# Two chunks of all four sequences in a group, instead of eight chunks of one sequence, in a chunked recurrence with a mixture of experts behind it

## The chip, the cores and the metric

The kernel runs on one core of a Trainium2 chip. The metric is the time of one execution on the device in microseconds; the median of three runs is compared.

## What is computed

A complex linear recurrence with a decay for each channel, read out by a query, and a mixture of experts with one expert per token behind it. Cut to what matters:

```python
B, H, S, D = 4, 8, 768, 48
scale = min(mag, 0.999) / (mag + 1e-6)          # mag = |a_re + i a_im|
for t in range(S):
    S_re, S_im = ar * S_re - ai * S_im + k[t] v[t]^T, ar * S_im + ai * S_re
    y[t] = q[t] @ S_re                           # for each sequence b and head h
x = y as 3072 tokens of 384
# 8 experts of 384 -> 1024 -> 384, argmax gate, capacity 768 rows an expert
out[i] = gate[i] * relu(x[i] @ w1[e]) @ w2[e]
```

## The kernel before

**Chunks.** Each sequence is cut into 8 chunks of 96 positions. Inside a chunk the products of decays from the chunk's middle outward are made by a scan; queries and keys are multiplied by them, and the chunk is then a small attention (scores, mask, times values) plus the contribution of a state `z` from the chunks before. A new state is made for the next chunk: S (keys times values, on TensorE) plus the old `z`, then a complex multiplication by the decay across the two chunk halves.

**Groups and stages.** The scan works on 128 partitions at once. These hold one group: one sequence, its 8 heads times 8 chunks, forward and backward from the middle (2 x 64 rows). A group has 6 tiles of 8 positions. `norm` (L246 on) loads `a` and normalises it, `scan` does two VectorE instructions a position (L362, L367), `post` (L381 on) multiplies the queries and keys and writes them to `scr` in DRAM. `pend` (L454 on) takes the decay at the scan's end, transposes it and makes `pcol`, the decays from one chunk to the next (L498 to L503). Stage g is the time of group g's scan.

**Units.** While group g+1 is scanned, the 8 chunks of group g go through `unit` (L507 on), one after the other. A unit loads `qkc` back from `scr` in two parts (480 KB and 90 KB, L524), the centre row and `v`, transposes (L542), makes the scores `pa` (L558), masks them to `a_sb` (L562), makes y (L614, and L619 with the state), and passes y to the router. For the state it does S (L572), the add on VectorE (L579 for the first chunk, L581 else), a copy of the sum with its partition halves swapped, as two transfers issued by SP (L585, tile `sx`), eight small multiplications on ScalarE (L590, tile `u`), `sx` times `pcol` on VectorE (L593, the update's first half) and their sum into the next state (L596, second half). The add of chunk c+1 reads the state made by chunk c.

**Routing and experts.** When a group's units are through, its tokens get experts and slots (`routing`), and their rows are sent to `disp`. In the last group this is done after 5 units and then unit by unit. Then the first expert's inputs are put together (L912, L918), and the experts run (L1032, L1040).

**The order.** Nearly all of this is recorded as operations of a planner (`Plan`): each has an engine, an estimated duration, the operations it comes after, the buffers it needs and a time `want` at which it is wanted. `solve` goes through them greedily and writes an order for each engine; the hardware then runs each engine's instructions in that order, so that one that waits holds up all behind it on its engine. The landing of a transfer is estimated in `solve` from its size and the queue (`o.lat`). `RINGS` has the number of buffers for each kind of tile, `BEGIN` the planned beginnings of the stages.

```python
x = [plan.op(None, "SP", .55, lambda i=i: swap(i), w - 20, after=[d], ..., kb=72) for i in range(2)]
u = plan.op(None, "ACT", 1.8, turn, w + 4 * f, after=[d, ("pc", b)], ...)
za = plan.op(None, "DVE", dve(384), state_a, w + 5 * f, after=x + [("pc", b)], ...)
plan.op(K("ZB"), "DVE", dve(384), state_b, w + 6 * f, after=[u, za], ...)
```

Here `d` is the add, `w` the time planned for the unit and `f` a ninth of the time planned for one unit.

Of the kernel before, what the change touches and what calls it, by code (L numbers as in the profile page):

```python
# [7 lines left out]
F32 = mybir.dt.float32  # L8
# [13 lines left out]
NC = S // C  # L22
SIZES = (8,) * 6
# [22 lines left out]
class Plan:  # L46
# [25 lines left out]
    def solve(self, slack=.13, late=8.):  # L72
# [30 lines left out]
        while left:  # L103
# [52 lines left out]
class Att:  # L156


    def __init__(self, const, c_att, tc, dram, ident, av, xv, cen, vp):
# [10 lines left out]
        self.sums = [const.tile([128, 2, NSUM], F32, name=f"sums{g}") for g in range(B)]  # L170
# [4 lines left out]
        for t in self.sums:  # L175
# [16 lines left out]
        self.col = [0] * B  # L192
# [53 lines left out]
    def norm(self, g, j, s0):  # L246
# [16 lines left out]
        plan.op(K + ("load",), eng, .6, load, w - 14, bufs=[a_], kb=48 * n)  # L263
# [117 lines left out]
    def post(self, g, j, e0):  # L381
# [11 lines left out]
        plan.op(K + ("load",), "POOL" if g else "SP", .6, load, w - 14, bufs=[i_], kb=48 * n)  # L393
# [60 lines left out]
    def pend(self, g, want):  # L454
# [31 lines left out]
        def copy():  # L486
            vg = st['vg'] = self.p_t.tile([C, 2, 2, H, NC], F32, tag="vg", name=f"vg_{g}", bufs=1)
            nc.scalar.copy(out=vg.rearrange("p z s h c -> p (z s h c)"), in_=st['pt'][:, :256])
        o = plan.op(None, "ACT", act(256), copy, want, after=[o], bufs=[("tr", K)])

        def cols():
            vg = st['vg']
            pr = self.p_t.tile([C, 2, H, NC], F32, tag="vgp", name=f"vgp_{g}", bufs=1)
            p = self.pcol[g]
            s1, s0 = slice(1, NC), slice(0, NC - 1)
            V = lambda z: vg[:, z, 0, :, s1]
            G = lambda z: vg[:, z, 1, :, s0]
# [3 lines left out]
            nc.vector.tensor_tensor(out=pr[:, 1, :, s1], in0=V(0), in1=G(1), op=ALU.mult)
            nc.vector.tensor_tensor(out=p[:, 0, :, s1], in0=p[:, 0, :, s1], in1=pr[:, 0, :, s1], op=ALU.add)
            nc.vector.tensor_tensor(out=p[:, 1, :, s1], in0=p[:, 1, :, s1], in1=pr[:, 1, :, s1], op=ALU.subtract)  # L503
        plan.op(("pc", g), "DVE", 6 * dve(56) + .2, cols, want + 2, after=[o])
# [914 lines left out]
```

## Time and profile before

| | us |
|---|---|
| median of three runs (725.82 to 727.86) | 727.04 |
| the profiled execution | 719.15 |
| its span, first to last instruction | 717.4 |
| TensorE matmul busy | 598.5 (83%) |
| VectorE busy | 468.8 (65%) |
| ScalarE busy | 383.4 (53%) |
| GpSimd busy | 160.1 (22%) |

All rows come from the profiled execution. Times in it count from the span's start. PE is TensorE's matmuls, PEld its weight loads, DVE VectorE, ACT ScalarE, POOL GpSimd, SP the engine that issues most transfers; a q behind a name is that engine's sequencer, which issues transfers. A busy share of the whole run mixes stages with different limits, so the stretches have to be looked at one by one.

### The profile page before, as it was taken

What the parts mean: (1) busy time and instruction counts of PE and PEld (TensorE: products, weight loads), DVE (VectorE), ACT (ScalarE), POOL (GpSimd) and SP (SyncE); (2) the same over time, 40 slices, a digit from 0 to 9 for tenths busy, and PEclk for the clock granted to TensorE, in tenths of its full rate; (3) what the DMA queues carried; (4) which work ended last, traced back from release to release, by engine and by line L of the source; (5) the groups of instructions that cost most, each with busy time, mean ns of one, the idle gap of its engine ahead of it and who ended that gap; (6) DMA issues with size and microseconds to landing.
All of it is one profiled execution on the core that took longest, in us unless ns stands there. A gap on an engine that the chain in (4) does not pass through costs nothing. (4 is left out here: it accounts for less than half of the span.)

```text
span 717.4 us, 12886 instructions
## 1 busy us (share of the span) xinstructions
PE 598.5 (83%) x4545; PEld 506.4 (71%) x4545; DVE 468.8 (65%) x1369; ACT 383.4 (53%) x1002; POOL 160.1 (22%) x231
## 2 busy tenths in 40 slices
PE   4445487968997777979658998999999999999994
PEld 1222176856886556767558886899999999999993
DVE  4999976878997886978635454345437454554721
ACT  7655475867786685767428642333426334352610
POOL 8124331122261221711212021002021111202012
PEclk9565578998999988989858988999999999999998
DMA  5368986767887666775688512643026707261601
GB/s 176 88 205 237 272 252 201 188 152 186 199 248 207 155 167 146 203 229 136 151 182 218 138 54 73 194 129 127 13 66 194 224 28 225 65 193 55 203 25 39
DMA packets 75929, 111.92 MB, mean 156 GB/s; under 512 B 7739, under 2 KB 65970, under 8 KB 75856
## 3 DMA queue, kind: packets, MB, share of 16 engines
q1 hardware_dynamic: 61904, 63.17, 32.8%
q0 software_dynamic: 13952, 47.84, 23.3%
q8 instruction: 38, 0.62, 0.4%
q14 instruction: 35, 0.29, 0.1%
HBM read 73.18 MB, written 34.46 MB: 150 GB/s over the span
## 5 line engine op out<-in xcount | busy, mean ns | idle before, releaser
L958 DVE TENSOR_TENSOR lo<-raw,hi 128x384 fp32r<-128x384 f32 (+2 forms) x128 | 65.0, 554 | 43.5 <-ACT hi L957 43.3
L1077 DVE SCALAR_TENSOR_TENSOR hl<-ph,hh 128x448 fp32r<-128x448 f32 x64 | 39.9, 623 | 70.7 <-ACT hh L1076 70.7
L957 ACT CAST hi<-raw 128x384 fp32r<-128x384 f32 (+2 forms) x128 | 59.0, 512 | 50.3 <-DMA raw<-in_moe_w_dram 27.7
L1076 ACT ACTIVATE hh<-ph 128x448 fp32r<-128x448 f32 x64 | 34.2, 545 | 88.1 <-PE ph L1032 88.0
L542 PE MATMUL tr<-ident,qkc 96*96 96x96 f32 x512 | 63.9, 265 | 20.7 <-issue 6.4
L240 PE MATMUL n<-a,ident 128*128 128x384 f32 x92 | 48.4, 665 | 35.7 <-ACT a L268 33.6
L542 PEld LDWEIGHTS tr<-ident,qkc 96*96 96x96 f32 x512 | 50.6, 136 | 28.8 <-issue 13.9
L1032 PE MATMUL ph<-xl,hi 128*128 128x448 f32 x192 | 70.6, 368 | 0.0
L1032 PE MATMUL ph<-xh,hi 128*128 128x448 f32 x192 | 70.5, 372 | 0.0
L1032 PE MATMUL ph<-xh,lo 128*128 128x448 f32 x192 | 69.9, 364 | 0.0
L240 PE MATMUL p<-qko,ident 128*128 128x384 f32 x96 | 47.5, 629 | 23.3 <-ACT qko L399 23.3
L1006 POOL DMA_INDIRECT out_dram<-o,xr x28 | 26.3, 941 | 180.2 <-DVE o L1005 175.9
L558 PE MATMUL pa<-qT,kT 128*96 128x96 f32 x512 | 58.5, 262 | 6.7 <-ACT kT L546 5.4
L362 DVE TENSOR_TENSOR xy<-a 128x192 f32<-128x192 f32 (+1 forms) x215 | 62.0, 306 | 1.6 <-ACT a L332 1.5
L590 ACT ACTIVATE u<-s,pcol 96x48 f32<-96x48 f32 x224 | 53.6, 324 | 16.8 <-DVE s L581 15.8
L1040 PE MATMUL my<-hh,lo 128*128 128x448 f32 x168 | 61.2, 364 | 0.0
L1040 PE MATMUL my<-hl,hi 128*128 128x448 f32 x168 | 61.1, 364 | 0.0
L558 PEld LDWEIGHTS pa<-qT,kT 128*96 128x96 f32 x512 | 53.2, 177 | 10.2 <-ACT kT L546 6.4
L240 PEld LDWEIGHTS n<-a,ident 128*128 128x128 f32 x92 | 21.1, 251 | 53.0 <-ACT a L268 35.2
L1040 PE MATMUL my<-hh,hi 128*128 128x448 f32 x168 | 56.0, 372 | 0.0
L614 PE MATMUL y<-a_sb,v 128*64 128x96 f32 x512 | 45.1, 266 | 12.6 <-DVE a_sb L562 12.6
L859 POOL DMA_INDIRECT disp<-x,idx x32 | 34.1, 1067 | 89.5 <-DVE sx L593 41.6
(192 smaller groups left out, 1374.4 us busy)
## 6 DMA issues: line engine op xcount, KB each, us to landing
raw<-in_moe_w_dram SPq DMA_DIRECT2D x64, 384.0 KB
qkc<-scr SPq DMA_DIRECT2D x32, 480.0 KB
scr<-qko POOLq DMA_DIRECT2D x24, 384.0 KB, 4.0
scr<-qko POOLq DMA_DIRECT2D x40, 192.0 KB, 5.3
a<-in_av_dram POOLq DMA_DIRECT2D x18, 384.0 KB, 5.5
qkin<-in_xv_dram POOLq DMA_DIRECT2D x18, 384.0 KB, 7.7
disp<-fill POOLq DMA_DIRECT2D x7, 772.0 KB, 8.7
xr<-disp SPq DMA_DIRECT2D x8, 675.5 KB
```

The lines of the kernel that those rows point to most:

```text
L240: nc.tensor.matmul(out=pt[:, :m], lhsT=self.ident, rhs=t[:, h:h + m], start=i == 0, stop=i == 1)
L362: nc.vector.tensor_tensor(out=st['xy'][:, :, cs].rearrange("p (u z) d -> p u z d", u=2), in0=a4[:, s, :, cs].rearrange("p (u z) d -> p u z ...
L542: nc.tensor.transpose(out=pt[:, h * C:h * C + C], in_=qk[:C, 4 * hh + h, z_ * C:z_ * C + C], identity=self.ident[:C, :C])
L558: nc.tensor.matmul(out=pa[:, h * C:h * C + C], lhsT=kT[:, 4 * hh + h], rhs=qT[:, 4 * hh + h], start=True, stop=True)
L590: nc.scalar.mul(out=u[:, h, :], in_=st['s'][:, h, :], mul=pc[:, 0, h, c + 1:c + 2])
L614: nc.tensor.matmul(out=py[o:o + DP, i // 2 * C:i // 2 * C + C], lhsT=v[:, h * D:h * D + DP], rhs=a_sb[:, h, :], start=True, stop=c == 0)
L957: return (lambda: nc.scalar.copy(out=hi[i][:, s], in_=raw[i][:, s]), lambda: nc.vector.tensor_tensor(out=lo[i][:, s], in0=raw[i][:, s], in ...
L958: lambda: nc.vector.tensor_tensor(out=lo[i][:, s], in0=raw[i][:, s], in1=hi[i][:, s].bitcast(F32), op=ALU.subtract))
L1032: nc.tensor.matmul(out=ph[:, :T], lhsT=a[:, k, fs], rhs=r[:, k], start=k == 0 and i == 0, stop=k == KT - 1 and i == 2)
L1040: nc.tensor.matmul(out=py[m][:, :T], lhsT=a[:, f % self.PF, ms], rhs=r, start=f == 0 and i == 0, stop=f == NF - 1 and i == 2)
L1076: nc.scalar.activation(hh, ph[:, :T], AF.Relu)
L1077: nc.vector.scalar_tensor_tensor(out=hl, in0=ph[:, :T], scalar=0.0, in1=hh.bitcast(F32), op0=ALU.max, op1=ALU.subtract)
```

## The change

A group no longer holds 8 chunks of one sequence but 2 chunks of all 4 sequences (group g has chunks 2g and 2g+1). The inputs are laid out for that on the host, as before for the old grouping. The units of a group go chunk 2g of the sequences 0 to 3 first and then chunk 2g+1 of the same. The state from chunk 2g+1 to 2g+2 needs the decays of two groups; its add, swap and S are done with the unit, and the two multiplications and the sum are finished in the next group's stage, after its scan. `pend` therefore makes `pcol` for each chunk of the group apart, with the tile `vg` of the group before. More states are kept: `z` has 6 buffers, the sum `s_sb` and its swapped copy `sx` 5 each; for this `a` and `qk` have 3 instead of 4, and `a4` has 4 instead of 5. The planner now counts 5 us more for the landing of a swap, 2 us more for the loads of `a` and `qk`, and 1 us more for those of `qkc`. Routing and the list of tokens follow the new order of units.

```diff
+NG = 4
+G2 = NC // NG
+NU = B * G2
-                o.lat = pipe[o.eng] + .5 - t - o.dur
+                o.lat = pipe[o.eng] + .5 + o.extra - t - o.dur
-        plan.op(K + ("load",), eng, .6, load, w - 14, bufs=[a_], kb=48 * n)
+        plan.op(K + ("load",), eng, .6, load, w - 14, bufs=[a_], kb=48 * n, extra=2.)
 def cols():
-            nc.vector.tensor_tensor(out=p[:, 0, :, s1], in0=V(0), in1=G(0), op=ALU.mult)
...
+            for i in range(int(g == 0), G2):
+                V = [self.vg[g][:, z, 0, :, i] for z in range(2)]
+                G = [self.vg[g - (i == 0)][:, z, 1, :, (i - 1) % G2] for z in range(2)]
+                p = [self.pcol[g][:, z, :, i] for z in range(2)]
+                nc.vector.tensor_tensor(out=p[0], in0=V[0], in1=G[0], op=ALU.mult)
...
-    def unit(self, b, c, w, per):
+    def unit(self, g, i, w, per, near):
-        n = NC * b + c
+        n = NU * g + i
+        b, c = i % B, G2 * g + i // B
+        zi = lambda c: (c - 1) * B + b
+        z, zn = buf("z", zi(c)), buf("z", zi(c + 1))
...
-            x = [plan.op(None, "SP", .55, lambda i=i: swap(i), w - 20, after=[d], bufs=[R("s_sb"), R("sx")], kb=72) for i in range(2)]
-            u = plan.op(None, "ACT", 1.8, turn, w + 4 * f, after=[d, ("pc", b)], bufs=[R("s_sb"), R("u")])
-            za = plan.op(None, "DVE", dve(384), state_a, w + 5 * f, after=x + [("pc", b)], bufs=[R("sx")])
-            plan.op(K("ZB"), "DVE", dve(384), state_b, w + 6 * f, after=[u, za], bufs=[R("sx"), R("u"), ("z", b, c + 1)])
+            x = [plan.op(None, "SP", .55, lambda i=i: swap(i), w - 20, after=[d], bufs=[R("s_sb"), R("sx")], kb=72, extra=5.) for i in range(2)]
+            pcn = ("pc", nx // G2)
+            wz = w + 12 * f if nx // G2 == g else near + 1.5 * b
+            u = plan.op(None, "ACT", 1.8, turn, wz, after=[d, pcn], bufs=[R("s_sb"), R("u")])
+            za = plan.op(None, "DVE", dve(384), state_a, wz, after=x + [pcn], bufs=[R("sx")])
+            plan.op(K("ZB"), "DVE", dve(384), state_b, wz + 2, after=[u, za], bufs=[R("sx"), R("u"), ("z", b, c + 1)])
...
-RINGS = dict(qkc=3, v=3, qT=3, kT=2, a_sb=2, z=3, s_sb=2, sx=2, u=2, xt=2, tr=2, pa=2, s=1, ad=2, y=1,
-             a=4, qk=4, a4=5, ln=4, c0=3, t5=3, xy=4, qko=4, pend=1)
+RINGS = dict(qkc=3, v=3, qT=3, kT=2, a_sb=2, z=6, s_sb=5, sx=5, u=2, xt=2, tr=2, pa=2, s=1, ad=2, y=1,
+             a=3, qk=3, a4=4, ln=4, c0=3, t5=3, xy=4, qko=4, pend=1)
...
+        for g in range(NG):
+            per = (BEGIN[g + 2] - BEGIN[g + 1]) / NU if g < NG - 1 else 7.05
+            for i in range(NU):
+                att.unit(g, i, BEGIN[g + 1] + 12 + per * i, per, BEGIN[min(g + 2, NG)] + 4)
```

The planner's order changes nearly everywhere. Three places matter here. Names carry first the sequence and the chunk for tiles of units (`s_1_4`: sequence 1, chunk 4), the group and the tile or position for tiles of the scan, and last a running number.

**VectorE, stage 2: from the add to the update's first half.** Before, sequence 1, chunk 4:

```order
L581 TENSOR_TENSOR s_1_4_2564<-s_1_4_2481,z1_126 96x384
L362 TENSOR_TENSOR xy_2_4_7_2574<-a4_2_4_2061,a4_2_3_1899 128x192
L562 TENSOR_TENSOR a_sb0_123<-pa_1_4_0_2558,mask_252 96x384
L367 TENSOR_TENSOR a4_2_4_2061<-xy_2_4_7_2574 128x2x24 x2
L362 TENSOR_TENSOR xy_2_4_6_2594<-a4_2_4_2061 128x4x24 x2
L367 TENSOR_TENSOR a4_2_4_2061<-xy_2_4_6_2594 128x2x24 x2
L562 TENSOR_TENSOR a_sb0_123<-pa_1_4_1_2585,mask_252 96x384
L362 TENSOR_TENSOR xy_2_4_5_2607<-a4_2_4_2061 128x192
L404 TENSOR_TENSOR qko_2_3_2581<-a4_2_3_1899,qkin_2_3_2320 128x8x96
L1255 TENSOR_SCALAR ok2_5405<-sums2_81 128x24
L367 TENSOR_TENSOR a4_2_4_2061<-xy_2_4_5_2607 128x96
L593 TENSOR_TENSOR sx_1_4_2565<-sx_1_4_2565,pcol1_109 96x384
```

In the changed kernel, chunk 2 of sequences 2 and 1:

```order
L586 TENSOR_TENSOR s_2_2_2355<-s_2_2_2263,z0_125 96x384
L323 SCALAR_TENSOR_TENSOR a4_2_3_1888<-a_2_3_1811,sign_93,t5n_2_3_1968 128x8x48
L598 TENSOR_TENSOR sx_1_2_2181<-sx_1_2_2181,pcol1_109 96x384
L327 TENSOR_TENSOR a4_2_3_1888<-a_2_3_1811,t5n_2_3_1968 128x8x48
L567 TENSOR_TENSOR a_sb0_123<-pa_2_2_0_2327,mask_254 96x384
L567 TENSOR_TENSOR a_sb0_123<-pa_2_2_1_2349,mask_254 96x384
L601 TENSOR_TENSOR z3_128<-u_1_2_2233,sx_1_2_2181 96x384
```

Before, the first half (L593) stands 11 rows behind the add of the same unit. In the changed kernel the add of sequence 2 (L586) is followed by the first half of sequence 1 (L598), whose own add stands 26 rows above; that of sequence 2 stands 21 rows below its add. Over stages 1 to 3 the distance is 7 to 13 rows before, with one of 27 (21 cases), and 16 to 94 in the changed kernel, median 44 (24 cases).

**VectorE, the last group: adds and updates.** Before, sequence 3, chunks 0 and 1:

```order
L579 COPY s_3_0_4406<-s_3_0_4375 96x384
L855 CAST idx_2_0_4365<-slot_2_0_4352 96x1 x2
L562 TENSOR_TENSOR a_sb0_123<-pa_3_0_0_4449,mask_252 96x384
L958 TENSOR_TENSOR lo1_0_0_4283<-raw1_0_0_4279,hi1_0_0_4281 128x384 x2
L562 TENSOR_TENSOR a_sb0_123<-pa_3_0_1_4471,mask_252 96x384
L593 TENSOR_TENSOR sx_3_0_4407<-sx_3_0_4407,pcol3_111 96x384
L596 TENSOR_TENSOR z0_125<-u_3_0_4431,sx_3_0_4407 96x384
L581 TENSOR_TENSOR s_3_1_4531<-s_3_1_4420,z0_125 96x384
```

In the changed kernel, chunk 6 of sequences 1, 0, 2 and 3:

```order
L586 TENSOR_TENSOR s_1_6_4589<-s_1_6_4525,z3_128 96x384
L867 CAST idx_2_0_4553<-slot_2_0_4540 96x1 x5
L970 TENSOR_TENSOR lo1_0_1_4365<-raw1_0_1_4361,hi1_0_1_4363 128x384 x2
L598 TENSOR_TENSOR sx_0_6_4467<-sx_0_6_4467,pcol3_111 96x384
L601 TENSOR_TENSOR z0_125<-u_0_6_4489,sx_0_6_4467 96x384
L586 TENSOR_TENSOR s_2_6_4658<-s_2_6_4609,z4_129 96x384
L970 TENSOR_TENSOR lo0_0_2_4412<-raw0_0_2_4408,hi0_0_2_4410 128x256
L567 TENSOR_TENSOR a_sb1_124<-pa_1_6_0_4653,mask_254 96x384
L970 TENSOR_TENSOR lo1_0_2_4413<-raw1_0_2_4409,hi1_0_2_4411 128x384 x2
L567 TENSOR_TENSOR a_sb1_124<-pa_1_6_1_4678,mask_254 96x384
L586 TENSOR_TENSOR s_3_6_4747<-s_3_6_4712,z5_130 96x384
```

Before, the next add (L581) reads the state `z0` that the row above it has made. In the changed kernel the adds read `z3`, `z4` and `z5`, which were finished before the group's units began; the state `z0` made here is for chunk 7.

**SP, the loads of the last group's first units and the first expert weights.** `qkc` from `scr3_1` is the large part, which needs the first five tiles of the group, from `scr3_0` the small part, which needs the last one; `raw` are weights, which go where the scan's tiles were and so wait for the scan's last transfers. Before:

```order
L948 DMA raw0_0_0_4278<-in_moe_w1_dram 128x3x256
L528 DMA qkc2_114<-in_cen_dram 1x1536
L948 DMA raw0_0_1_4297<-in_moe_w1_dram 128x3x256
L524 DMA qkc2_114<-scr3_1_103 80x8x192
L524 DMA qkc0_112<-scr3_0_102 15x8x192
```

In the changed kernel:

```order
L533 DMA qkc2_114<-in_cen_dram 1x1536
L529 DMA qkc2_114<-scr3_1_103 80x8x192
L960 DMA raw0_0_0_4353<-in_moe_w1_dram 128x3x256
L960 DMA raw0_0_1_4360<-in_moe_w1_dram 128x3x256
L536 DMA v2_117<-in_vp_dram 96x384
L529 DMA qkc0_112<-scr3_0_102 15x8x192
```

The third unit's large part has moved ahead of the weights, out of the place between them and the first unit's small part.

## Rows read from the trace of the kernel before

**Rows 1.** Busy time by engine in seven stretches of the span: begin and end, length, busy us and number of instructions of PE, PEld, DVE, ACT and POOL, then the granted TensorE clock (1.00 is 2.4 GHz), the busy share of the DMA engines and GB/s. The first three are stages 1 to 3, then the gap before the tail, the tail, the first expert's inputs, the experts.

```profile
71.10:159.60 88.50, 65.84 (x617) 52.03 (x617) 70.43 (x234) 57.14 (x160) 22.07 (x32) 0.83 0.79 216
159.60:253.80 94.20, 81.09 (x842) 65.88 (x842) 81.82 (x251) 71.67 (x206) 30.52 (x40) 0.93 0.75 195
253.80:345.70 91.90, 76.55 (x800) 62.35 (x798) 77.08 (x245) 63.76 (x182) 26.94 (x34) 0.90 0.66 171
345.70:371.20 25.50, 13.12 (x114) 10.89 (x110) 12.19 (x45) 6.42 (x20) 2.61 (x4) 0.65 0.78 174
371.20:440.70 69.50, 62.65 (x744) 57.07 (x745) 36.20 (x131) 40.89 (x132) 15.12 (x15) 0.88 0.54 136
440.70:454.00 13.30, 13.30 (x49) 8.23 (x48) 2.86 (x19) 1.09 (x3) 0.92 (x1) 0.74 0.41 106
454.00:717.00 263.00, 252.97 (x1346) 234.66 (x1344) 127.03 (x242) 98.02 (x212) 31.38 (x32) 0.99 0.38 117
```

**Rows 2.** The timeline of ScalarE, the copy at the end of each scan (start, duration).

```profile
71.06 0.26 ACT L464 COPY pend<-a 128x96 f32<-128x96 f32 x1
...
159.57 0.28 ACT L464 COPY pend<-a 128x96 f32<-128x96 f32 x1
...
253.84 0.26 ACT L464 COPY pend<-a 128x96 f32<-128x96 f32 x1
...
345.65 0.25 ACT L464 COPY pend<-a 128x96 f32<-128x96 f32 x1
```

**Rows 3.** Who VectorE waited for, in three stretches (72 to 163, 163 to 254 and 254 to 350 us): us in total, times, the longest.

```profile
DVE sx L593 <- DMA sx<-s: 13.4, 3, 6.6
...
DVE sx L593 <- DMA sx<-s: 7.3, 3, 3.7
...
DVE sx L593 <- DMA sx<-s: 8.9, 4, 4.1
DVE s L579 <- PE s L572: 5.6, 1, 5.6
```

**Rows 4.** The instructions that write or read the swapped copy: duration least, median and most in ns, first and last start; and what VectorE waited for before them.

```profile
L593 DVE TENSOR_TENSOR sx<-sx,pcol x28: 541/553/555, 102.3 to 423.8; 96x384 f32<-96x384 f32 x28
L596 DVE TENSOR_TENSOR z<-u,sx x28: 542/554/614, 103.0 to 424.3; 96x384 f32<-96x384 f32 x28
...
  DMA sx<-s: 35.3, 12
```

**Rows 5.** The timelines of SP and VectorE around two swaps (start, duration, in brackets the wait before).

```profile
100.60 1.24 SPq L524 DMA_DIRECT2D qkc<-scr  x2
...
104.24 1.63 SPq L585 DMA_DIRECT2D sx<-s  x2
...
103.66 0.55 DVE L581 TENSOR_TENSOR s<-s,z 96x384 f32<-96x384 f32 x1
...
113.89 0.55 DVE L593 TENSOR_TENSOR sx<-sx,pcol 96x384 f32<-96x384 f32 x1 [6.57 <-DMA sx<-s]
...
249.40 1.89 SPq L585 DMA_DIRECT2D sx<-s  x2
...
254.31 0.55 DVE L593 TENSOR_TENSOR sx<-sx,pcol 96x384 f32<-96x384 f32 x1 [1.70 <-DMA sx<-s]
```

**Rows 6.** Transfers by source, with the size of each.

```profile
qkc<-scr SPq DMA_DIRECT2D x32, 480.0 KB
...
sx<-s SPq DMA_DIRECT2D x56, 72.0 KB
qkc<-scr SPq DMA_DIRECT2D x32, 90.0 KB
```

**Rows 7.** The eight multiplications in the list of groups (busy us, mean ns, idle before), and two `pcol` instructions in VectorE's timeline.

```profile
L590 ACT ACTIVATE u<-s,pcol 96x48 f32<-96x48 f32 x224 | 53.6, 324 | 16.8 <-DVE s L581 15.8
...
350.88 0.20 DVE L498 TENSOR_TENSOR pcol<-vg 96x56 f32<-96x56 f32 x1
351.00 0.20 DVE L499 TENSOR_TENSOR pcol<-vg 96x56 f32<-96x56 f32 x1
```

**Rows 8.** The chain of states in the tail, from the timelines of VectorE and SP.

```profile
401.15 0.55 DVE L581 TENSOR_TENSOR s<-s,z 96x384 f32<-96x384 f32 x1
...
401.73 1.15 SPq L585 DMA_DIRECT2D sx<-s  x2
...
405.94 0.56 DVE L593 TENSOR_TENSOR sx<-sx,pcol 96x384 f32<-96x384 f32 x1 [3.77 <-DMA sx<-s]
406.60 0.55 DVE L596 TENSOR_TENSOR z<-u,sx 96x384 f32<-96x384 f32 x1
407.26 0.55 DVE L581 TENSOR_TENSOR s<-s,z 96x384 f32<-96x384 f32 x1
...
412.07 0.55 DVE L581 TENSOR_TENSOR s<-s,z 96x384 f32<-96x384 f32 x1
...
418.22 0.55 DVE L581 TENSOR_TENSOR s<-s,z 96x384 f32<-96x384 f32 x1
```

**Rows 9.** TensorE's groups in the tail (371.2 to 440.7 us): S, and y with the state.

```profile
L572 PE MATMUL s<-v,qkc 128*96 128x96 f32 x112 | 12.6, 275 | 0.0
...
L619 PE MATMUL y<-qT,z 128*48 128x96 f32 x112 | 9.3, 246 | 0.0
```

**Rows 10.** From the last scan's end to the tail, from the timelines of VectorE, GpSimd, SP and TensorE.

```profile
353.82 0.94 DVE L436 TENSOR_TENSOR qko<-a,v 128x768 f32<-128x768 f32 x1
...
355.06 0.56 POOL L444 DMA_DIRECT2D scr<-qko  x1 [3.93 <-DVE qko L436]
355.61 0.77 POOL L447 DMA_DIRECT2D scr<-qko  x1
...
359.86 0.40 SPq L948 DMA_DIRECT2D raw<-in_moe_w_dram  x1
...
361.14 1.49 SPq L524 DMA_DIRECT2D qkc<-scr  x3
...
371.25 0.84 PE L542 MATMUL tr<-ident,qkc 96*96 96x96 f32 x4 [6.42 <-issue]
```

**Rows 11.** The norm's first square, of which the last one opens the last tile.

```profile
L268 ACT ACTIVATE a<-a x24: 826/842/868, 4.7 to 319.0; 128x768 f32<-128x768 f32 x24
```

More of the change, by code (lines that the diff above doesn't have):

```diff
@@ L168, in __init__ @@
         make_identity(nc, self.ident)
-        self.sums = [const.tile([128, 2, NSUM], F32, name=f"sums{g}") for g in range(B)]
+        self.sums = [const.tile([128, 2, NSUM], F32, name=f"sums{g}") for g in range(NG)]
         self.b_lncap = const.tile([128, 1], F32, name="b_lncap")
@@ L184, in __init__ @@
         self.scr = [[dram.tile([64, n, 4 * D], F32, name=f"scr{g}_{i}") for i, n in enumerate((NF_, NR))]
-                    for g in range(B)]
-        self.small = [const.tile([128, 1], F32, name=f"small{g}") for g in range(B)]
-        self.pcol = [const.tile([C, 2, H, NC], F32, name=f"pcol{g}") for g in range(B)]
+                    for g in range(NG)]
+        self.small = [const.tile([128, 1], F32, name=f"small{g}") for g in range(NG)]
+        self.pcol = [const.tile([C, 2, B, G2, H], F32, name=f"pcol{g}") for g in range(NG)]
+        self.vg = {}
         self.bufs = {}
@@ L501, in cols @@
[L501 to L504, printed above, removed]
-    def unit(self, b, c, w, per):
+            pr = self.p_t.tile([C, 2, B, H], F32, tag="vgp", name=f"vgp_{g}", bufs=1)
@@ L644, in routing @@
         W = n * E_
-        gs = [("u", b, i, x) for i in range(c0, c + 1) for x in ("G", "X")]
+        gs = [("u", i % B, G2 * b + i // B, x) for i in range(c0, c + 1) for x in ("G", "X")]
         s = span / 8
@@ L1247, in uncovered @@
 def uncovered(nc, const, ps, sums, smalls, route):
-    bad = const.tile([128, B + 2], F32, name="bad")
+    bad = const.tile([128, NG + 2], F32, name="bad")
     nc.vector.memset(bad, 0.0)
-    for g in range(B):
+    for g in range(NG):
         ok = const.tile([128, 2, NSUM], F32, name=f"ok{g}")
@@ L1262, in uncovered @@
     nc.vector.tensor_reduce(out=m, in_=route.fine, op=ALU.min, axis=AX.X)
-    nc.vector.tensor_scalar(out=bad[:C, B:B + 1], in0=m, scalar1=-1.0, scalar2=1.0, op0=ALU.mult, op1=ALU.add)
-    nc.vector.tensor_reduce(out=bad[:C, B + 1:B + 2], in_=route.over, op=ALU.max, axis=AX.X)
+    nc.vector.tensor_scalar(out=bad[:C, NG:NG + 1], in0=m, scalar1=-1.0, scalar2=1.0, op0=ALU.mult, op1=ALU.add)
+    nc.vector.tensor_reduce(out=bad[:C, NG + 1:NG + 2], in_=route.over, op=ALU.max, axis=AX.X)
     one = const.tile([128, 1], F32, name="one")
@@ L1267, in uncovered @@
     pb = ps.tile([C, 512], F32, tag="tr", name="pbad", bufs=2)
-    nc.tensor.matmul(out=pb[0:1, :B + 2], lhsT=one, rhs=bad, start=True, stop=True)
+    nc.tensor.matmul(out=pb[0:1, :NG + 2], lhsT=one, rhs=bad, start=True, stop=True)
     flag = const.tile([1, 1], F32, name="flagf")
-    nc.vector.tensor_reduce(out=flag, in_=pb[0:1, :B + 2], op=ALU.add, axis=AX.X)
+    nc.vector.tensor_reduce(out=flag, in_=pb[0:1, :NG + 2], op=ALU.add, axis=AX.X)
     nc.vector.tensor_scalar(out=flag, in0=flag, scalar1=1.0, scalar2=None, op0=ALU.min)
@@ L1290 @@
         plan = att.plan
-        wants = [[BEGIN[g] + (BEGIN[g + 1] - BEGIN[g]) * (M - 1 - v) / M for v in range(M)] for g in range(B)]
-        for g in range(B):
+        wants = [[BEGIN[g] + (BEGIN[g + 1] - BEGIN[g]) * (M - 1 - v) / M for v in range(M)] for g in range(NG)]
+        for g in range(NG):
             for j in range(NS):
@@ L1298 @@
         early = len(plan.ops)
-        for b in range(B):
-            per = (BEGIN[b + 2] - BEGIN[b + 1]) / 8 if b < B - 1 else 7.05
-            for c in range(NC):
-                att.unit(b, c, BEGIN[b + 1] + 12 + per * c, per)
+        for g in range(NG):
+            per = (BEGIN[g + 2] - BEGIN[g + 1]) / NU if g < NG - 1 else 7.05
+            for i in range(NU):
+                att.unit(g, i, BEGIN[g + 1] + 12 + per * i, per, BEGIN[min(g + 2, NG)] + 4)
         box = {}
@@ L1341, in moe_plan @@
     done = list(plan.ops[:early])
-    t0 = BEGIN[B] + 8
+    t0 = BEGIN[NG] + 8
     w = {}
```

70 lines of the change are left out of this document (36 added, 34 removed).

## The prediction

> **What bounds the kernel now.** I read the profile by stages. The four copies that end each scan [rows 2] cut the span: scan 0 ends at 71.1 us, the next ones at 159.6, 253.8 and 345.7. After the last scan come a gap, the eight units of the last group (the tail), the first expert's inputs, and from 454 us the experts. The table of busy time by engine for these stretches [rows 1] shows two different limits.
>
> In stages 1 to 3 (88.5, 94.2 and 91.9 us) VectorE is the fullest engine: 70.4, 81.8 and 77.1 us, so 18.1, 12.4 and 14.8 us idle. The list of who waited for whom on VectorE says for what [rows 3]: 13.4, 7.3 and 8.9 us went into one line, the first half of the state update (L593), which waits for the swapped copy `sx`; 29.6 us of the 35.3 us that this line waits in the whole run [rows 4]. A wait on VectorE stops the scan too, since the scan's steps stand behind it in the same queue. The timeline of one such wait [rows 5]: the add (L581) starts at 103.66, SP issues the two swaps at 104.24, right behind 570 KB of `qkc` loads [rows 6] issued at 100.60, and L593 starts only at 113.89, 9.65 us after the issue. The shortest of the waiting ones here: issue 249.40, start 254.31, 4.9 us. A swap takes 4.9 to 9.7 us, and the old order gives it about ten VectorE rows, at 81.82 us for 251 instructions some 3.3 us.
>
> In the tail (371.2 to 440.7 us) the units form a chain: add 401.15, swap 401.73, state update 405.94 and 406.60, next add 407.26 [rows 8]. That is 6.1 us from add to add, and 6.15 us again from 412.07 to 418.22. TensorE is busy 62.65 of 69.5 us [rows 1], so chain and TensorE bind nearly alike. From 454 us on the experts keep TensorE busy 253 of 263 us; the change does not touch them.
>
> **The change, part by part.**
>
> Distance of the swap. By the order, rows from add to L593 go from 7 to 13 (20 of 21 cases in stages 1 to 3, one 27) to 16 to 94, with a median of 44, some 14 us by the price above. Only four of 24 have fewer than 24 rows, 5.3 to 7.3 us, and may still wait. Were all waits gone, 29.6 us would go; were none, 0. I take 70%, 20.7 us: a wait nearly always ends inside the new distance, but four cases stay short, and TensorE and ScalarE, which now run beside a waiting VectorE, must keep pace (below).
>
> A rule speaks against this gain. The Trainium skill, DMA: Bandwidth & Descriptors, section "Anatomy of one DMA — SWDGE (gpsimd) path", fits a transfer as about 2.0 us plus its bytes at 436 GB/s; for 72 KB that would be an estimated 2.2 us, less than the old distance, and no swap would ever have been waited for. The rows show 4.9 to 9.7 us for swaps issued by SP behind other loads, so the measurement decides.
>
> More VectorE work in stages 1 to 3. Three more adds (21 to 24; a sequence's last chunk has none, and all four of those now stand in the tail), 0.55 us each [rows 5]: +1.65. One state update fewer, two instructions of 0.55 us [rows 4]: -1.1. The columns `pcol` take twelve more instructions, at 0.12 us from one start to the next [rows 7]: +1.5. Sum +2.0 us. ScalarE's eight multiplications per update (53.6 us for 224, so 1.9 us an update [rows 7]) are 28 updates before and after.
>
> The tail. Only the four units of chunk 6 still make a state; the others have neither S nor update, and four chains of one link replace one of seven. S takes 12.6 us for 112 instructions [rows 9], 1.8 us a unit; three units fewer: -5.4. The first unit now has a state behind it and so a second y product, 9.3 us for 112 [rows 9], 1.3 us: +1.3. Together -4.1 us of TensorE work, which is the lower end. TensorE's idle 6.85 us in the tail is mostly the chain's; the upper end takes all of it, -11. I take -8.3, a little over half of the idle time, since routing (logits, count, place) still links the last three units.
>
> The tail's start. The first transposes begin 25.6 us after the scan's end: the last `qko` is made at 353.82, leaves at 355.06 and 355.61, SP reaches the weights at 359.86 and the loads at 361.14, and the data is there at 371.25 [rows 10]. In the new order one load of 480 KB [rows 6] goes ahead of the weights instead of between them and the last part; at 174 GB/s [rows 1] that is up to -2.8 us. Against it, up to six `pcol` instructions, three first halves and one second half of updates stand ahead of the last `qko` on VectorE, 6 x 0.12 + 4 x 0.55 = +2.9 us, and the second half also waits for ScalarE. I take 0 and keep both ends. ScalarE's four updates (7.6 us) fit into the 25.6 us in which the loads are out; without that cover the first unit would start up to 7.6 us later.
>
> Fewer buffers for `a`, `qk` and `a4` I cost at nothing. A slot of `a4` is held from the norm's first square (319.0, the last of L268) to the last `qko` (353.82), some 36 us [rows 10, 11]; four slots at a tile every 91.9/6 = 15.3 us allow 61 us, and at a shortened 13.7 us still 55. The two state-row rings grow, and the planner's later landing times move loads earlier, which costs nothing by itself.
>
> Sum: -20.7 + 2.0 - 8.3 = **-27.0 us**. The profiled execution took 719.15 us and would take 692.2. The median of the three runs is 727.04, 7.9 above it, for which the rows show no place; I carry that along: **700.0 us**.
>
> **The rivals.**
>
> (a) *TensorE takes over in the stages.* It is busy 81.1 of 94.2 us in stage 2, and gets one S and one y more (3.1 us): 84.2. If VectorE runs ahead it will wait for `pa` or the sums instead. If a third of the waits' time is kept: -9.9 + 2.0 - 4.1 = -12.0, **715**. For it: 86% busy. Against it: weight loads are busy 65.9 of 94.2 us [rows 1], 70%. The Trainium skill, Trace Analysis, section "Identifying the Most-Contended Engine", holds weight-load time to be the better measure of the two and matmul time a bad one; by it this rival would be weaker than I price it, and no row here decides.
>
> (b) *Everything goes:* all 29.6 us, also the 5.6 us that the first add of stage 3 waits for S [rows 3], and the tail's upper end: -29.6 - 5.6 + 2.0 - 11 = -44.2, **683**.
>
> (c) *The waits move and don't shrink:* if L593's waits come from what SP and the rings carry in that stretch (DMA engines 66 to 79% busy in the stages [rows 1]) and not from the short distance, another instruction will wait there in its place, a load's user perhaps. Only the tail's -8.3 is left: **719**. The fit of the Trainium skill (DMA: Bandwidth & Descriptors) above, with its 2.2 us, would come out here. Against it: every wait is booked on `sx` itself, straight behind its issue.
>
> (d) *Slower: four slots of `a4` starve the scan.* The place is the norm's first square, which needs a slot that the post work of four tiles earlier has left. It decides once a slot is held for over 55 us. Then each of 18 tiles loses time: at 2 us a tile +36, so with the forecast's -27 it is +9, **736**. Against it: 36 us today.
>
> (e) *No difference,* within 0.3% (2.2 us, about what a measurement of this kernel can tell from no change): the gain is eaten by later units. By VectorE's rows this needs all terms at their bad ends.
>
> **How the numbers follow.** Forecast 0.56, (a) 0.15, (b) 0.12, (c) 0.06, (d) 0.07, (e) 0.04. The forecast's own range, with 50 to 90% of the waits gone, tail -4 to -11 and tail start -2.8 to +2.9, is about 690 to 711. The range from 686 to 719 takes in (a) and (c) and part of (b), and leaves out (d), (e) and the rest of (b), under 0.2. Faster: 0.56 + 0.15 + 0.12 + 0.06 = 0.89; the same 0.04; slower 0.07.
>
> **What would show it.** Right: waits of the state update's first half in stages 1 to 3 under 9 us in sum; stages 1 to 3 ending some 19 us earlier in the span; add to add in the tail no longer 6 us apart by a swap, and the tail near 61 us; the experts' 263 us unchanged. Wrong: VectorE idle as before but waiting for `pa`, for the sums or for `u` (rival a); ScalarE's first square waiting for a slot (d); the first transposes of the tail later than 28 us after the scan's end, or stages as long as before with the swap waits gone.

## The result, and the profile after

The changed kernel takes 703.9 us (median of four runs, 702.7 to 708.7), the kernel before beside it 726.4; the ratio is 0.9709, 95% interval 0.965 to 0.9769. Forecast were 700.0 us and 686 to 719. The profiled execution took 702.66 us against 719.15, 16.5 us less where the sum said 27.0; the medians lie 22.5 apart. The total came out nearly right. The term for the tail did not, and the two traces differ in more than the kernel, as the signals of TensorE show below.

The same seven stretches as in [rows 1], in the same columns, for the changed kernel:

```profile
70.47:152.72 82.25, 67.67 (x614) 52.03 (x614) 72.32 (x231) 58.58 (x157) 23.18 (x34) 0.83 0.87 239
152.72:244.41 91.69, 80.20 (x852) 66.50 (x848) 80.93 (x258) 68.78 (x199) 29.12 (x39) 0.93 0.78 196
244.41:331.34 86.93, 74.17 (x784) 60.73 (x785) 77.02 (x245) 63.69 (x185) 25.30 (x33) 0.94 0.68 181
331.34:352.90 21.56, 12.63 (x135) 10.25 (x133) 12.79 (x40) 13.81 (x52) 2.59 (x4) 0.70 0.85 213
352.90:422.61 69.71, 59.30 (x731) 53.24 (x731) 34.72 (x143) 35.87 (x109) 15.50 (x15) 0.92 0.52 134
422.61:437.22 14.61, 14.61 (x48) 9.26 (x48) 2.71 (x16) 1.09 (x3) 0.92 (x1) 0.67 0.23 54
437.22:700.90 263.68, 253.45 (x1346) 234.50 (x1344) 126.86 (x242) 98.15 (x212) 31.35 (x32) 0.99 0.39 119
```

Stages 1 to 3 lose 6.3, 2.5 and 5.0 us, the gap 3.9. The tail keeps its length, though TensorE has 3.4 us less to do in it; its idle time there rises from 6.85 to 10.4 us.

Who VectorE waited for in the three stages, one after the other (answers to [rows 3]; us, times, longest), and at the end all waits for the swapped copy (answers to [rows 4]):

```profile
DVE s L584 <- PE s L577: 4.4, 1, 4.4
DVE sx L598 <- DMA sx<-s: 2.1, 2, 1.7
...
DVE a_sb L567 <- PE tr L547: 7.2, 1, 7.2
DVE s L586 <- PE s L577: 2.7, 1, 2.7
...
DVE s L586 <- PE s L577: 4.7, 1, 4.7
DVE a_sb L567 <- PE tr L547: 3.6, 2, 1.9
...
  DMA sx<-s: 2.1, 2
```

The waits that the change was to remove are gone, 2.1 us where 35.3 stood. In their place VectorE waits for the units' sums and, before it can mask, for their scores; the longest of these waits takes 7.2 us, in stage 2.

The tail, read at the copy of each unit's y (ScalarE). Before:

```profile
382.02 0.48 ACT L745 COPY xt<-y 128x384 f32<-128x384 f32 x1
389.64 0.47 ACT L745 COPY xt<-y 128x384 f32<-128x384 f32 x1
398.10 0.48 ACT L745 COPY xt<-y 128x384 f32<-128x384 f32 x1 [1.54 <-PE y L619]
405.71 0.48 ACT L745 COPY xt<-y 128x384 f32<-128x384 f32 x1 [0.92 <-PE y L619]
411.33 0.48 ACT L745 COPY xt<-y 128x384 f32<-128x384 f32 x1 [0.65 <-PE y L619]
418.71 0.48 ACT L745 COPY xt<-y 128x384 f32<-128x384 f32 x1 [2.42 <-PE y L619]
430.97 0.48 ACT L745 COPY xt<-y 128x384 f32<-128x384 f32 x1 [1.51 <-PE y L619]
437.20 0.48 ACT L745 COPY xt<-y 128x384 f32<-128x384 f32 x1 [2.34 <-PE y L619]
```

In the changed kernel:

```profile
363.83 0.48 ACT L757 COPY xt<-y 128x384 f32<-128x384 f32 x1 [1.57 <-PE y L628]
377.05 0.48 ACT L757 COPY xt<-y 128x384 f32<-128x384 f32 x1 [3.23 <-PE tr L547]
383.69 0.46 ACT L757 COPY xt<-y 128x384 f32<-128x384 f32 x1
388.14 0.48 ACT L757 COPY xt<-y 128x384 f32<-128x384 f32 x1 [1.01 <-PE y L628]
393.30 0.48 ACT L757 COPY xt<-y 128x384 f32<-128x384 f32 x1 [1.01 <-PE y L628]
398.91 0.48 ACT L757 COPY xt<-y 128x384 f32<-128x384 f32 x1 [1.35 <-PE y L628]
411.00 0.48 ACT L757 COPY xt<-y 128x384 f32<-128x384 f32 x1 [5.63 <-remote]
418.80 0.48 ACT L757 COPY xt<-y 128x384 f32<-128x384 f32 x1 [2.34 <-PE y L628]
```

Units 3 to 6 come 4.4 to 5.6 us apart; before, the distances were 7.6, 8.5, 7.6, 5.6, 7.4, 12.3 and 6.2. So the chain of states no longer sets the pace. But unit 2 comes 13.2 us after unit 1, and unit 7 comes 12.1 us after unit 6. Both gaps end at or just after a burst of indirect sends on GpSimd (the transfers that take rows to `disp`). The second one, GpSimd first, then TensorE, ScalarE and VectorE:

```profile
403.68 0.92 POOL L871 DMA_INDIRECT disp<-x,idx  x1 [27.82 <-DVE mx L817]
...
408.56 0.92 POOL L871 DMA_INDIRECT disp<-x,idx  x1 [0.30 <-issue]
...
405.94 0.34 PE L628 MATMUL y<-qT,z 128*48 128x96 f32 x4
...
411.53 0.45 PE L781 MATMUL y<-xt,wg 128*32 128x96 f32 x8 [4.45 <-ACT xt L757]
...
411.61 0.16 DVE L841 TENSOR_REDUCE se<-lm 96x1 f32<-96x8 f32 x1 [6.68 <-ACT lm L835]
```

The y that ScalarE copies is done at 406.28, yet the copy starts at 411.00, 1.5 us after the last send's issue is over (409.48). No instruction that ends there releases it, hence "remote". The 7.2 us in stage 2 look the same: sends from 186.19 to 196.15, one unit's scores (`pa`) finished at 189.64 and the next one's at 195.75, the mask of the first only at 197.88.

```profile
186.19 0.99 POOL L871 DMA_INDIRECT disp<-x,idx  x1 [4.79 <-DVE idx L867]
...
195.23 0.92 POOL L871 DMA_INDIRECT disp<-x,idx  x1 [0.30 <-issue]
...
188.80 0.84 PE L563 MATMUL pa<-qT,kT 128*96 128x96 f32 x8
...
194.16 1.59 PE L563 MATMUL pa<-qT,kT 128*96 128x96 f32 x8 [2.33 <-issue]
...
197.88 0.55 DVE L567 TENSOR_TENSOR a_sb<-pa,mask 96x384 f32<-96x384 f32 x1 [7.25 <-PE tr L547]
```

The traces also record when each signal of an engine to the others (an update of a semaphore) arrives, and these times show what the rows do not print. TensorE's signal for the y that ended at 406.28 arrives at 410.92, and its next two, for work ended at 406.71 and 407.08, at 410.98 and 411.04. The signal for the scores of 189.64 arrives at 197.86, and the mask starts 0.02 us later. In this trace 26 of some 615 signals of TensorE come more than 0.5 us after their work has ended, up to 8.2 us, all of them beside bursts of sends; of those recorded for ScalarE and VectorE none does. In the trace of the kernel before not one is late: the largest delay is 0.04 us, beside four bursts of the same 29 sends. So the two traces differ in this too, and a comparison of them stretch by stretch charges late signals to one side alone.

**Theory:** the regrouping did what was forecast, and late signals beside bursts of sends took part of it back. **Rivals:** the planner's new landing times alone make the gain; the first loads of a stage are what VectorE now waits for; the tail is bound by something other than the bursts; the late signals come with the chip and not with the program.

### The profile page after: what moved, and what is told of

Same layout as the page of the kernel before. It is cut to its first block, busy times and chain, and to the rows that moved or that the text cites. A ratio compares the mean times of both kernels' runs of the same rounds, so it can differ in the third digit from the quotient of the medians.

```text
span 700.9 us, 12902 instructions
## 1 busy us (share of the span) xinstructions
PE 591.5 (84%) x4545; PEld 500.7 (71%) x4545; DVE 467.3 (67%) x1383; ACT 384.2 (55%) x1002; POOL 159.7 (23%) x234
## 4 chain that ended last, share of the span: by engine, by line
PE 47%; DVE 25%; issue 10%; DMA 10%; ACT 4%; POOL 2%; another core or an unknown queue 1%; SPq 0%; DVEq 0%; POOLq 0%; ACTq 0%
PE ph L1044 14%; PE my L1052 13%; DVE xy L367 5%; DMA scr<-qko 5%; PE tr L547 4%; DVE a L372 3%; DMA qkc<-scr 3%; PE pa L563 3%; PE s L577 3%; DVE qko L441 2%; DMA sx<-s 2%; DVE qko L409 2%; DVE a_sb L567 1%; PE mt L924 1%; PE n L245 1%
## 5 line engine op out<-in xcount | busy, mean ns | idle before, releaser
L969 ACT CAST hi<-raw 128x384 fp32r<-128x384 f32 (+2 forms) x128 | 59.0, 512 | 49.0 <-DMA raw<-in_moe_w_dram 26.7
L547 PE MATMUL tr<-ident,qkc 96*96 96x96 f32 x512 | 62.3, 259 | 17.2 <-DMA qkc<-scr 7.9
L245 PE MATMUL n<-a,ident 128*128 128x384 f32 x92 | 46.4, 641 | 35.1 <-ACT a L273 29.4
L547 PEld LDWEIGHTS tr<-ident,qkc 96*96 96x96 f32 x512 | 49.1, 133 | 25.1 <-issue 12.7
L563 PE MATMUL pa<-qT,kT 128*96 128x96 f32 x512 | 57.0, 256 | 8.7 <-ACT kT L551 5.1
L563 PEld LDWEIGHTS pa<-qT,kT 128*96 128x96 f32 x512 | 51.0, 170 | 11.8 <-ACT kT L551 7.2
L245 PE MATMUL p<-qko,ident 128*128 128x384 f32 x96 | 43.1, 578 | 18.9 <-ACT qko L404 18.9
L567 DVE TENSOR_TENSOR a_sb<-pa,mask 96x384 f32<-96x384 f32 x64 | 35.1, 549 | 28.0 <-PE pa L563 15.1
L871 POOL DMA_INDIRECT disp<-x,idx x32 | 32.5, 1016 | 87.5 <-DVE idx L867 33.1
```

The lines of the kernel that those rows point to most:

```text
L245: nc.tensor.matmul(out=pt[:, :m], lhsT=self.ident, rhs=t[:, h:h + m], start=i == 0, stop=i == 1)
L547: nc.tensor.transpose(out=pt[:, h * C:h * C + C], in_=qk[:C, 4 * hh + h, z_ * C:z_ * C + C], identity=self.ident[:C, :C])
L563: nc.tensor.matmul(out=pa[:, h * C:h * C + C], lhsT=kT[:, 4 * hh + h], rhs=qT[:, 4 * hh + h], start=True, stop=True)
L567: nc.vector.tensor_tensor(out=a_sb[:C, 4 * hh:4 * hh + 4, :], in0=st[hh][:, :4 * C].rearrange("p (h t) -> p h t", h=4), in1=self.mask.unsq ...
L969: return (lambda: nc.scalar.copy(out=hi[i][:, s], in_=raw[i][:, s]), lambda: nc.vector.tensor_tensor(out=lo[i][:, s], in0=raw[i][:, s], in ...
```

## The experiments

Three groups of four kernels, each group on one chip beside the kernel before (medians 723.2, 711.4 and 724.5 us there). The first group (`again` to `qkc_later`) and the third (`after_side` on) have chip number 6, the second (`after_no_sends` to `rings_only`) has chip 0; for the first two traces no chip is on record. Ratios are against the kernel before of the same group. Stretches of each profiled execution, in us, from the scans' ends, the tail's first transposes and the first expert's inputs as in the windows above; "rest" begins with these inputs, and stage 0 (70.1 to 71.5 us) is not in the table. "Late" counts TensorE's signals that arrive more than 0.5 us after their work has ended, of some 600 in each trace:

| kernel | median | ratio (95%) | stages 1-3 | gap | tail | rest | late |
|---|---|---|---|---|---|---|---|
| before (first trace) | 726.4 | 1 | 274.6 | 25.6 | 69.4 | 276.7 | 0 |
| changed (first trace) | 703.9 | 0.971 (0.965-0.977) | 260.9 | 21.6 | 69.7 | 278.3 | 26 |
| again | 704.3 | 0.975 (0.968-0.982) | 259.2 | 21.8 | 71.4 | 278.4 | 26 |
| no_numbers | 704.8 | 0.976 (0.969-0.982) | 256.7 | 23.6 | 73.0 | 278.4 | 22 |
| numbers_only | 732.2 | 1.012 (1.008-1.016) | 260.2 | 27.3 | 89.1 | 282.1 | 20 |
| qkc_later | 710.3 | 0.983 (0.976-0.989) | 265.4 | 26.0 | 72.9 | 276.8 | 18 |
| after_no_sends | 681.5 | 0.960 (0.956-0.964) | 252.3 | 21.7 | 59.3 | 276.7 | 0 |
| before_no_sends | 710.0 | 0.997 (0.992-1.001) | 275.0 | 25.5 | 65.1 | 275.5 | 0 |
| spread | 685.3 | 0.965 (0.962-0.968) | 249.0 | 25.4 | 62.1 | 276.0 | 0 |
| rings_only | 708.7 | 0.996 (0.993-1.000) | 270.8 | 22.6 | 68.7 | 279.1 | 0 |
| after_side | 704.2 | 0.974 (0.971-0.976) | 259.4 | 21.3 | 71.3 | 279.7 | 26 |
| spread_side | 686.7 | 0.950 (0.946-0.954) | 247.9 | 25.3 | 62.9 | 277.8 | 3 |
| before_spread | 708.6 | 0.977 (0.973-0.981) | 267.6 | 24.5 | 66.4 | 281.2 | 0 |
| spread_no_numbers | 684.1 | 0.945 (0.943-0.948) | 250.8 | 24.3 | 63.5 | 275.4 | 8 |

Six traces have 18 to 26 late signals, all beside back-to-back bursts; one of them, `numbers_only`, has the old grouping. On chip 0 none is late, in three traces with bursts as dense as these and in one with the sends apart. Chip 0 is also where the kernel before takes 711.4 us.

**The changed kernel once more** (`again`, no edit).

> The changed kernel once more, unedited. Its profiled execution has a standstill of ScalarE of 5.6 us at 405 us in the tail (TensorE waits 4.5 us and VectorE 6.7 us with it) that no instruction of the trace releases, while GpSimd issues five sends. Theory A: it belongs to the program (the sends or what they load); then it comes again within 1 us of the same place and the tail is again 69 to 70 us. Theory B: it is chance; then it is gone or elsewhere, and the tail is 64 to 66 us. Time 702 to 709 either way.

The standstill is back: ScalarE waits 5.65 us for the same copy, until 409.90, 1.50 us after the burst. The mask in stage 2 waits 7.3 us again. The tail takes 71.4 us, a little over what theory A said. So it is not chance on this chip; that it needs nothing but the program does not follow, as chip 0 shows.

**Regrouping without the new landing times** (`no_numbers`).

```diff
-... kb=72, extra=5.)     # likewise extra=2. and extra=1. of the loads
+... kb=72, extra=0.00)
```

> The changed kernel with the planner's later landings taken out (0 instead of 5, 2 and 1 us), the new grouping kept. Theory A, the regrouping makes the distance: waits for the swapped copy in stages 1 to 3 stay under 6 us and the time is 702 to 709. Theory B, the planner's numbers make it: the waits for the copy come back with 10 us or more, 712 to 720.

The time is that of the changed kernel, and the waits for the copy stay at 6.0 us in all: theory A, the regrouping alone makes the distance.

**The landing times without regrouping** (`numbers_only`).

```diff
-... kb=72)               # in the kernel before; likewise 2 and 1 us for the loads
+... kb=72, extra=5.)
```

> The kernel before with only the planner's later landings (5 us for a swap, 2 for a and qk, 1 for qkc), old grouping. The distance from add to first half then is about 22 rows instead of 10. Theory A, the chain of seven states binds: the copy's waits shrink from 29.6 us to some 10, but the next add and the y product stand later, and the tail is as long as before: 716 to 724. Theory B, the numbers are what brings the gain in the stages: 708 to 714.

Both theories fell short. The stages gain as much as in the changed kernel (260.2), with 1.4 us of waits left; but the tail grows to 89.1 us and the whole is slower than before. The tail on VectorE shows why:

```profile
427.00 0.55 DVE L582 TENSOR_TENSOR s<-s,z 96x384 f32<-96x384 f32 x1
434.62 0.55 DVE L594 TENSOR_TENSOR sx<-sx,pcol 96x384 f32<-96x384 f32 x1
435.21 0.55 DVE L597 TENSOR_TENSOR z<-u,sx 96x384 f32<-96x384 f32 x1
435.79 0.55 DVE L582 TENSOR_TENSOR s<-s,z 96x384 f32<-96x384 f32 x1
```

From add to add it is now 8.8 us, against 6.1 in [rows 8]. Later placing lengthens every link of a chain of seven. Some of the 89.1 us is not the chain's: unit 1 comes 18.6 us after unit 0, beside a burst with four signals 6.1 to 7.0 us late. The regrouping is what makes distance free.

**Later loads for the units** (`qkc_later`).

```diff
-... kb=6 * NR, extra=1.)     # likewise for NF_
+... kb=6 * NR, extra=6.0)
```

> The changed kernel with 6 us instead of 1 us counted for the landing of qkc. In it VectorE waits in stages 1 to 3 some 24 us for the sums and the scores of the units, whose TensorE work comes right behind the loads of qkc. Theory A, these waits come from rows that are placed before their load has landed: they fall under 12 us, and the time is 690 to 698. Theory B, the loads' landing only moves with the order and the units then end later: the waits stay over 18 us or move to the tail's start, 702 to 708.

Slower than both theories said. The waits do not go: stage 2 has its 7.8 us beside the burst, stage 3 has 9.4 us for scores and sums. Gap and tail together take 98.9 us instead of 91.3. Counting later landings for these loads is no cure.

**The two late bursts left out** (`after_no_sends`, `before_no_sends`).

```diff
-... "POOL", 1.0, fs['send'][i], w + ...
+... "POOL", 1.0, (lambda: None) if (b, c + 1) in ((2, 8), (3, 5)) else fs['send'][i], w + ...
```

> The changed kernel without the eight sends of the third group's tokens and the five of the last group's first five units (they are left out, so those rows never reach the experts). In the changed kernel these two bursts run at 364.6 to 375.9 and 403.7 to 409.5 us, and the tail's units 1 to 2 and 6 to 7 lie 13.2 and 12.1 us apart where the units between take 4.4 to 6.6. Theory A, the bursts hold the other engines up: both distances fall to 6 or 7, and the tail (first transposes to first inputs of the expert) from 69.7 to 57 to 60 us, the time to 690 to 693. Theory B, loads or the first units' data set these distances: they stay over 10, the tail over 66, the time 698 to 704.

> The kernel before without the same thirteen sends. Its bursts run at 372.2 to 382.8, beside the tail's first unit, and 424.4 to 430.2; the units lie 7.6, 8.5, 7.6, 5.6, 7.4, 12.3 and 6.2 us apart. Theory A, the burst at the tail's start costs this kernel little, as it lies beside its first unit, and only the second one counts; the chain of states then still sets some 6 to 8 us from unit to unit: tail 62 to 65 us against 57 to 60 in the changed kernel, so without the bursts the regrouping shows its 5 to 8 us. Theory B: both kernels' tails shorten alike, 69.4 and 69.7 to the same length within 1.5 us, and the regrouping has gained nothing in the tail in itself.

The tails are nearly those of theory A, 59.3 and 65.1 us. Both kernels ran on chip 0, and neither trace has a late signal, so this pair shows what the regrouping is worth without them: 28.5 us between medians (710.0 and 681.5). The two traces lie 31.6 us apart, 22.7 of it in the stages, 3.8 in the gap and 5.8 in the tail.

What leaving out the sends does to either kernel is less clear. The changed kernel with its sends did not run on chip 0, so the fall of its two distances from 13.2 and 12.1 us to 8.8 and 7.5 mixes the sends with the chip, and its 681.5 us are below both theories. The kernel before gains 1.4 us in the median, which is not clear of noise, and its distance of 12.3 us beside the last burst stays at 11.4 without that burst.

The bursts of stages 2 and 3 were left in, and the order of the engines is that of the changed kernel. These two stages take 168.9 us here, against 177.3 to 178.6 in the three traces of the changed kernel, which have some 14 late signals in them; stage 1, which has no burst, is 1.2 to 1.6 us longer here. So 8 to 10 us go with the chip and its late signals, not with the order.

**Sends put apart** (`spread`, `spread_side`, `after_side`).

```diff
+            if o.apart is not None and o.apart.start is not None:
+                t = max(t, o.apart.start + 2.6)
...
-            x = plan.op(None, "DVE", .12, fs['cast'][i], w + (5 + i) * s, after=[o])
+            y = plan.op(None, "DVE", .12, fs['cast'][i], w + (5 + i) * s, after=[o, x])
+            y.apart, x = x, y
```

> The changed kernel, with the sends of one routing step put 2.6 us apart by the planner (the conversion of each index on VectorE, which a send waits for, is placed so far behind the one before it) instead of 1.2 us. Theory A, a standstill lasts as long as GpSimd issues sends back to back: it falls apart, the tail is 62 to 66 us and the time 694 to 700. Theory B, each send costs the other engines the same wherever it stands: the sum stays, tail 68 to 71, time 700 to 705. Slower is possible where the last sends then hold up the load of the first expert's inputs: 705 to 710.

> The changed kernel, on the chip of the next three. Theory A, the bursts of sends hold it up also here: tail 68 to 71 us against 62.1 in the kernel with the sends put apart, stages 2 and 3 together 175 to 179 against 165.8. Theory B, the other chip made the difference: tail and stages within 2 us of the kernel with the sends apart.

> The changed kernel with the sends 2.6 us apart, once more, beside the changed kernel itself. Theory A: 10 to 20 us less than the changed kernel of this chip. Theory B: within 3 us.

On chip 6 the changed kernel takes 704.2 us and the one with sends apart 686.7, 17.5 less. That is theory A for both runs. The two traces, 17.7 us apart, differ by 11.5 us in the stages, 8.4 in the tail and 1.9 in the rest, against 4.0 more in the gap. It beats both kernels; on chip 0 (`spread`, 685.3) it came out faster than either theory said. Late signals fall from 26 to 3, the longest 1.4 us. But the edit changes more than the sends: the planner also moves some 170 of VectorE's 1383 instructions and some 100 of ScalarE's 1002, and how much of the 17.5 us is due to that is open. Its units in the tail, ScalarE's copies:

```profile
356.77 0.48 ACT L761 COPY xt<-y 128x384 f32<-128x384 f32 x1
362.36 0.46 ACT L761 COPY xt<-y 128x384 f32<-128x384 f32 x1
...
384.24 0.48 ACT L761 COPY xt<-y 128x384 f32<-128x384 f32 x1 [1.35 <-PE y L630]
393.03 0.48 ACT L761 COPY xt<-y 128x384 f32<-128x384 f32 x1 [2.34 <-PE tr L549]
```

Unit 2 is 5.6 us behind unit 1, unit 7 is 8.8 behind unit 6, and no copy waits for "remote". All of VectorE's waits in stage 2:

```profile
DVE s L588 <- PE s L579: 1.7, 1, 1.7
DVE lnn L309 <- ACT lnn L300: 0.2, 1, 0.2
```

**Sends apart in the kernel before** (`before_spread`, the same edit).

> The kernel before with only the sends put 2.6 us apart, old grouping and old landing times. Its stages showed no standstill beside the bursts, only waits for the swapped copy. Theory A, a burst costs only where the units' work has no other room, so here it brings 0 to 6 us, and the regrouping with sends apart keeps 25 us or more of advantage. Theory B, it brings the same 10 to 17 us here as in the changed kernel.

My theory A fell here: it gains 15.9 us, nearly the 17.5 of the changed kernel. Its 708.6 us on chip 6 are about what the kernel before takes on chip 0 with its bursts (711.4). So on chip 6 the old order seems to pay for bursts too. The first trace, in which no single wait showed it, has no late signal; of the old grouping on chip 6 with its bursts there is only the trace of `numbers_only`, which has 20. Here too the planner moves instructions, some 220 of VectorE's, so the gain may not be the sends' alone. The advantage of the regrouping with sends apart is 21.9 us between medians, not 25 or more; between the two traces (spans 711.2 and 684.5) it is 26.7.

**Sends apart, no landing times** (`spread_no_numbers`).

> The changed kernel with the sends 2.6 us apart and the planner's later landings at 0. Without them the third scan ended 4.4 us earlier, but the tail was 3.3 us longer and its start 2 us later. Theory A, the longer tail came from a burst (its first unit took 20 us): with the sends apart 3 to 5 us less than with the landings. Theory B, the landings matter in the tail for themselves: the same within 2 us.

2.6 us less than with the landing times, between the two theories.

**Fewer buffers alone** (`rings_only`).

```diff
-             a=4, qk=4, a4=5,
+             a=3, qk=3, a4=4,
```

> The kernel before with only the smaller numbers of buffers: 3 instead of 4 for a and qk, 4 instead of 5 for a4. If slots of a4 starve the scan, 2 us a tile and some 36 us slower; if the smaller rings cost nothing, as in the sum of the prediction, within 3 us of the kernel before.

Within 3 us (708.7 and 711.4): the buffers cost nothing, and rival (d) has no ground.

## Why the prediction was right and where it was wrong

- **Distance of the swap (-20.7) and VectorE's work (+2.0).** The mechanism was right. The waits went from 29.6 to 2.1 us (of the 29.6, 2.7 lie behind the third scan's end, in the window's last us). Between the first two traces the stages got 13.7 us shorter, not 18.7, with 14 late signals in stages 2 and 3 of the second trace. Where both traces are free of late signals the stages differ by 19.7 us (sends apart, 267.6 to 247.9) and 22.7 us (late bursts left out, 275.0 to 252.3). So 70% was, if anything, a low price. VectorE's busy time in the stages rose by 0.9 us, not 2.0.
- **The tail (-8.3).** This is the term that failed: measured +0.3 between the first two traces, -3.5 with sends apart, -5.8 without the late bursts. Its first part was right in direction and near in size, TensorE's work at -3.4, -6.2 and -4.8 us against -4.1, and the chain is gone from units 3 to 6. The step that failed is the other one: I called TensorE's idle 6.85 us "mostly the chain's" and counted on over half of it. The idle time rose to 10.4 us in the first pair; with sends apart it rose too, from 6.5 to 9.3, and without the late bursts it fell only from 5.4 to 4.4. The trace of before had it already. TensorE's longest waits in that tail (371.3 to 440.7 us):

```profile
PE y L769 <- ACT xt L745: 2.6, 2, 2.0
PE pp L815 <- DVE se L829: 1.6, 1, 1.6
PE tr L542 <- ACT x L762: 1.0, 1, 1.0
```

  They are for ScalarE's copies and for the routing, and none of the shorter ones is for a state either. Routing's 1.6 us are still there in the changed kernel. In its trace 4.5 us of idle time are the late signal at 410.92, which holds up the copy of y; with sends apart 1.4 us for the count of tokens and 1.2 us for the first expert's inputs come in.
- **The tail's start (0, from -2.8 to +2.9).** Measured -4.0 in the first two traces and -3.8 without the late bursts, outside the range by about 1 us; +0.8 with sends apart. No run separates the loads from the instructions counted against them.
- **Rings (0).** Right, by `rings_only`.
- **What was not in the sum.** The first expert's inputs take 1.3 us longer, TensorE's clock being 0.67 there against 0.74 in [rows 1]; the experts 0.3 us longer, stage 0 0.6 shorter. Sum: -13.7 + 0.3 - 4.0 + 1.3 + 0.3 - 0.6 = -16.4, the trace's -16.5 within rounding. Late signals of TensorE were no term at all, and a trace without them could not have shown that one was needed.
- **The 7.9 us carried along.** The trace of before lay below its median, that of after hardly does (702.66 and 703.9). So the total hides some 6 us of the 10.5 by which the sum was off, and that 700.0 came so close to 703.9 is in part luck. That trace has no late signal, and its execution may have been faster for that reason; this is not shown, as the slower ones have no trace. Free of late signals on both sides, the regrouping is worth 28.5 us (late bursts left out) and 21.9 us (sends apart) between medians, on either side of the 27.0 of the sum.
- **Rivals.** (c), that another instruction waits in the swap's place, holds in part where signals are late, as the 7.2 us before the mask show; with sends apart VectorE waits 1.9 us in all of stage 2. (a) does not hold: with sends apart TensorE does the same work in stages of 82.8 and 81.1 us. The fit in the Trainium skill that the prediction holds against the gain (DMA: Bandwidth & Descriptors, section "Anatomy of one DMA — SWDGE (gpsimd) path") is one for transfers that GpSimd issues; the swaps are issued by SP, so it was no rule against them.

## What to carry to other kernels

A chain through a transfer is cured by putting independent links between its steps, not by placing the consumer later: that helps where the engine has other work and lengthens every link where it has not. Before a term counts on idle time going away, name each wait that it is made of. Before two traces are compared stretch by stretch, see that they are alike in what the kernel does not decide: here one had late signals and the other none. Putting a burst of sends a few us apart was worth nearly as much on chip 6 (17.5 us) as the rewrite (20.4).

## What the runs showed of the hardware

On some executions TensorE's signals to the other engines arrive late while GpSimd issues indirect sends back to back (one every 1.22 us, 0.30 us between them). In six traces, all with such bursts, 18 to 26 of some 600 signals come more than 0.5 us late, the latest by 7.6 to 8.7 us; no recorded signal of ScalarE or VectorE does. They come in batches, 0.06 us apart, while sends are still being issued or up to 2.3 us after the last one, and engines that wait start then; these started 1.5 to 1.7 us after it: 409.48 to 411.00 and 196.15 to 197.88 in the changed kernel, 408.40 to 409.90 in its second trace, 409.04 to 410.53 without landing times. With the sends 2.6 us apart in the plan, at most 8 signals are over 0.5 us late, none by more than 1.4.

Dense bursts are not enough. The first trace of before has none late, nor has any of the four traces of chip 0, with bursts as dense in three of them. That fits the kernel before taking 711 us there and 723 to 726 elsewhere, and the changed kernel taking about the same on both chips once its sends are apart (685.3 and 686.7). It is not shown, as the changed kernel itself did not run on chip 0. Why signals are late stays open: no run separated the issuing of descriptors, their transfers and the signals. The traces of chip 6 and the first one of the changed kernel also lack 38 to 89 of some 2660 records of signals, most of them beside sends, where the others lack at most one; so the recording itself may take part.

The Trainium skill, SBUF — State Buffer, section "SBUF: two separate sides", knows contention between engines only at the port that GpSimd and VectorE share, and holds that TensorE's and ScalarE's ports wait for nobody. Here ScalarE stood still for 5.6 us, but for a signal of TensorE and not at a port, so that rule does not name this cause.
